# Low parts of five weight pairs moved from VectorE to GpSimd, block 4's Gram run one slot later, and its L read by another queue

## The chip, the cores and the metric

The kernel runs on one core of a Trainium2 chip. The metric is device time in microseconds (us) of one execution; lower is better. Engines are called TensorE (PE; its weight loads are PEld), VectorE (DVE), ScalarE (ACT), GpSimd (POOL) and SyncE (SP). Each runs its own instructions strictly in order and meets the others through semaphores. SP, ACT and POOL also issue DMAs, each from its own queue.

## What is computed

Two stages, float32 throughout. The first is a delta-rule linear attention over 4 batches x 8 heads, 768 positions and head size 48; the second is a two-layer network on its output, 384 to 2048 and back.

```
k_n = k / (norm(k) + 1e-06)
for t in range(S):
    y[t] = q[t] @ state
    state = state + beta[t] * outer(k_n[t], v[t] - k_n[t] @ state)
h = x @ w_in          # x: y of all heads, (3072, 384)
out = maximum(0.01 * h, h) @ w_out
```

## The kernel before

**Tiling.** The 768 positions are cut into 12 blocks of 64. In a block all recurrences are independent, so a block of attention is dense algebra: the Gram products of its keys and queries (`gram`, TensorE tile `pg`, line 307), the inverse of a unit triangular matrix by column elimination on VectorE (`inv`, tiles `T`, `tmp` and `L`, lines 388 and 393), and small products that carry the state on (`solve`, tiles `pz`, `pu`, `pk`, `pw`, `py`, `pc`). The feed-forward part (`ffn`) works on the block before: 16 column groups f, two to a weight pair. For each f, nine matmuls make `ph` (line 722), ScalarE writes `gh` from it and VectorE the rest `gl` (line 737), and six matmuls add into `po` (line 713).

**High and low parts.** From block 1 on, a float32 product is made of three rounded ones: high x high, high x low, low x high. So each weight pair j (0 to 7) exists as a high part, rounded by ScalarE in `cast` (line 182), and a low part, the difference, made in `lows` (line 189) by one 128x1536 subtraction. Block 0 uses the plain weights. f 6 and 7 of block 1 need the low part of pair 3, f 8 and 9 that of pair 4, and so on to pair 7.

**Shared buffers.** The unrounded weights of pairs 3 and 4 lie in buffers `c3` and `c4`. `square` (line 478) takes the same two buffers for A and B, the block-diagonal tiles of `solve` from block 2 on: ScalarE zeroes them (tile `sq`, line 482) once the low parts of pairs 3 and 4 have been read. The elimination's result T goes to DRAM as `td` and, transposed by a ScalarE copy (line 453), as `tt`; it comes back as A (from `tt`, line 520), B (from `td`, line 523) and `rt` (line 529). `pz` multiplies by A, `pu` by B.

**What sets the order.** A hand-written loop at the end of the kernel emits the work: within block n and slot s (17 slots), first a step of `ffn`, then weight work from the table `work`, then steps of `solve`, `inv` and `gram`, spread over slot ranges in the tables `SV`, `IV`, `GG` and `G4`. A scheduler then orders each engine's instructions by a simulated timeline; `behind(name)` holds the instructions of its block that run on the marked instruction's own engine behind that instruction. In block n runs the `solve` of block n+1 and the `inv` of block n+2. Block 1 also holds two Grams, of blocks 3 and 4; the later blocks hold one.

**Lines that the change touches.** `lows` (185 to 194), `gram` (276 to 353; the DMA queue of block 4's Gram is chosen in line 290, `queue = nc.gpsimd if n == GS * NGR else nc.sync`) and the table `G4` (852). Names in the trace: `w<-cg,w` is a low part, `gd<-gs` and `L<-gd` carry a Gram's triangle through DRAM to the elimination, `kq` is a block's keys and queries, `rq` the masked queries, `gm` the corners, `rv` values and state.

Of the kernel before, what the change touches and what calls it, by code (L numbers as in the profile page):

```python
# [9 lines left out]
F32 = mybir.dt.float32  # L10
# [5 lines left out]
ALU = mybir.AluOpType  # L16
# [9 lines left out]
GS = 2  # L26
NGR = NSEQ // GS
# [20 lines left out]
def delta_moe_kernel(ctx: ExitStack, tc, kq0, kqT, kv, qT, beta, cst, w_all, out, nblk):  # L48
# [10 lines left out]
    nc = tc.nc  # L59
# [33 lines left out]
    def of(x, n, g):  # L93
        return ring[x][(n * NGR + g) % NR[x]]
# [23 lines left out]
    def behind(name):  # L118

        return tc.issue_after(mark[name]) if name in mark else nullcontext()  # L120
# [29 lines left out]
    def after(inst):  # L150
        mark["gl"] = mark["dv"] = inst.ins
# [33 lines left out]
    def lows(j):  # L185
        g, t = parts[j]
        hi, lo = t[:, 0:4 * DO], t[:, 4 * DO:]
        with behind("dv"), behind("el2" if j > 2 else None):
            after(nc.vector.tensor_tensor(lo, g, hi.bitcast(F32), ALU.subtract))  # L189
        for y, part in enumerate((hi, lo)):  # L190
            for e in range(2):
                for x, w in enumerate((wi, wo)):
                    w[y][2 * j + e] = part[:, (2 * e + x) * DO:(2 * e + x + 1) * DO]

    Lh, gm, nrm, Tts, zs, ys, xs, done = {}, {}, {}, {}, {}, {}, {}, set()

    def need(gen, fn, n):
        while (fn, n) not in done:
            next(gen)
# [76 lines left out]
    def gram(n):  # L276
        need(sv, solve, n - Q_BUFS // NGR)
        kqs = []
        for g in range(NGR):
            t = sb.tile([P, GS, NPAIR, 2, C], F32, tag="kq", name=f"kq{n}_{g}", bufs=KQ_BUFS)  # L280
            kqs.append(t)
            with behind("kq"):
                for b in range(2):
                    nc.sync.dma_start(t[b * R0:b * R0 + D].rearrange("p s u x t -> p (s u x t)"), kqT[n, g, b])
        if n == GS:
            yield
        b0 = where[n][0]
        Lh[b0] = sb.tile([P, HC, HC], F32, tag="L", name=f"L{b0}", bufs=2)
        gd = dr.tile([64, HC, HC], F32, tag="gd", name=f"gd{n}")
        queue = nc.gpsimd if n == GS * NGR else nc.sync  # L290
        if n - 1 > 1 and where[n - 1][0] in nrm:
            with behind("ph"):
                lengths(n - 1)
        for g in range(NGR):
            kq = kqs[g]
            gs = sb.tile([P, 2, NPAIR, C], F32, tag="gs", name=f"gs{n}_{g}", bufs=2)
            if not g:
                gm[n] = sb.tile([P, GU, HC], F32, tag="gm", name=f"gm{n}", bufs=GM_BUFS)

            ps = [ps_a.tile([P, 512], F32, tag="a", name=f"pg{n}_{g}_{b}") for b in range(2)]  # L300
            pv = [x.rearrange("p (u x t) -> p x u t", u=NPAIR, x=2) for x in ps]
            for p in range(NPAIR):
                for c in range(2):
                    for b in range(2):
                        r = slice(b * R0, b * R0 + D)
                        with behind("ph") if n > 2 else nullcontext():
                            nc.tensor.matmul(ps[b][c * 64:(c + 1) * 64, p * 128:(p + 1) * 128],  # L307
                                             kq[r, c ^ b, p, 0], kq[r, c ^ b, p].rearrange("p x t -> p (x t)"),
                                             start=True, stop=True)
            for b in range(2):  # L310
                nc.scalar.copy(gs[:, b], pv[b][:, 0])  # L311
            for c in range(2):
                for e in range(2):
                    a = e * HS + g * GH + c * GU
                    queue.dma_start(
                        gd[a:a + GU].rearrange("l j i -> j l i"),
                        gs[c * 64 + e * HC:c * 64 + (e + 1) * HC].rearrange("p b u t -> p (b u) t")[:, :, e * HC:(e + 1) * HC])

            def masked(pv=pv, qa=of("q", n, g)):
                for b in range(2):  # L320
                    for c in range(2):
                        r = slice(c * 64, (c + 1) * 64)
                        with behind("gl") if n > 2 else nullcontext():
                            nc.vector.tensor_tensor(  # L324
                                qa[DN, c, b * NPAIR:(b + 1) * NPAIR], pv[b][r, 1],
                                tri[r].rearrange("p (o t) -> p o t", o=1).broadcast_to([C, NPAIR, C]), ALU.mult)

            def corners(g=g, gs=gs):
                for c in range(2):
                    k = 2 * g + c  # L330
                    with behind("gl") if n > 2 else nullcontext():
                        nc.vector.tensor_copy(gm[n][k * HC:(k + 1) * HC].rearrange("p (b u) t -> p b u t", b=2), gs[c * 64:c * 64 + HC, :, :, HC:])

            if n == 2:
                masked()
                corners()
            elif not g:
                masked()
                held.append(corners)
            else:  # L340
                tails.extend([[masked], held + [corners]])
                held.clear()
            if g == NGR - 1:
                for r in range(2):
                    i = queue.dma_start(Lh[b0][r * 64:(r + 1) * 64].rearrange("l j i -> l (j i)"), gd.rearrange("l j i -> l (j i)"))
                if n == GS * NGR:
                    mark["kq"] = i.ins
                done.add((gram, n))
            yield
# [53 lines left out]
    def inv(b):  # L403

        if b:
            need(gg, gram, NB[b][0])
# [159 lines left out]
    def lengths(n):  # L566

        b, i = where[n]
        ps = ps_a.tile([P, 512], F32, tag="a", name=f"pn{n}")
        nc.tensor.matmul(ps[DN, 0:HS], nrm[b][i * 64:i * 64 + 64], eye0[i * 64:i * 64 + 64], start=True, stop=True)  # L570
        nt = nts[n] = sb.tile([P, NGR, 2, GU], F32, tag="nt", name=f"nt{n}", bufs=2)
        if n < 2:
            for y in range(2):
                nc.scalar.copy(nt[DN, :, :, y * NPAIR:(y + 1) * NPAIR],
                               ps[DN, y * GH:(y + 1) * GH].rearrange("p (g h v) -> p g h v", g=NGR, h=2))
        else:
            nc.scalar.copy(nt[DN].rearrange("p g h u -> p (g h u)"), ps[DN, 0:HS])
        if not n:
            for g in range(NGR):
                v = of("v", n, g)  # L580
                for u in range(GU):
                    for c in range(2):
                        nc.scalar.mul(v[DN, c, u], v[DN, c, u], nt[DN, g, c, u:u + 1])
# [190 lines left out]
    def weave_at(i, n, *streams):  # L774

        for gen, steps, a, b in streams:
            key = gen, n, a
            want = steps if i >= b - 1 else min(steps, max(0, i + 1 - a) * steps // (b - a))
            while taken.get(key, 0) < want:
                next(gen, None)  # L780
                taken[key] = taken.get(key, 0) + 1
# [5 lines left out]

    NS, NF, NI = NSLOT, NFC + 1, HC + 1
    fg, gg = first(), chain(gram, range(2, nblk))
    iv = chain(inv, range(len(NB)))  # L790
    sv = chain(solve, range(nblk))
# [19 lines left out]
    lo, hi = slice(0, 1), slice(1, 2)  # L811
# [3 lines left out]
    for j in (4, 5):  # L815
# [7 lines left out]
        2: ((load_w, 6, "dv"), (conv, 3), (final, 2), (pack, 4, "h0_2")),  # L823
        3: ((expand, 3, "h0_3"),),
        4: ((load_w, 7, "dv"), (conv, 4), (final, 3), (cast, 0, "h0_4"), (lows, 0)),
        5: ((expand, 4, "h0_5"), (pack, 5, "h0_4")),
        6: ((conv, 5), (final, 4), (cast, 1, "h0_6"), (lows, 1)),
        7: ((expand, 5, "h0_7"), (pack, 6, "h0_6")),
        8: ((conv, 6), (final, 5), (cast, 2, "h0_8"), (lows, 2)),
        9: ((expand, 6, "h0_9"), (pack, 7, "h0_8")),  # L830
        10: ((conv, 7), (final, 6),),
# [5 lines left out]
    for n in range(nblk):  # L837

        for s in range(NF):
            at = min(n, 3)  # L840
            weave_at(s, n, (ff, NF, 0, NF))
            for fn, *args in work.pop(n * NF + s, ()):
                fn(*args)
            weave_at(s, n, (sv, (NS + (n == 0)) * (n + 1 < nblk), *SV[at]), (iv, NI * (n + 2 < nblk), *IV[at]),
                     (gg, NGR * (n < 2), *GG[min(n, 1)]), (gg, NGR * (0 < n < nblk - 3), *G4[min(n, 2)]))

# [2 lines left out]
WARM = {HC - 12: 16}  # L849
KA = 2  # L850
IV, GG = ((9, 17), (6, 17), (2, 17), (2, 17)), ((2, 4), (1, 2))
G4 = (0, 1), (13, 14), (12, 13)
SV = (0, 10), (3, 13), (1, 11), (2, 12)
PD, FB = 2, 4

# [65 lines left out]
```

## Time and profile before

| | |
|---|---|
| median of 3 runs | 621.96 us (621.48 to 624.78) |
| the profiled execution | 626.66 us, its span 624.7 us |
| PE busy | 584.0 us (93%) |
| PEld busy | 537.3 us (86%) |
| DVE busy | 431.4 us (69%) |
| ACT busy | 330.6 us (53%) |
| POOL busy | 39.5 us (6%) |

The span runs from the first to the last instruction; the execution's own time is 2.0 us longer. Busy shares are means over stages with different limits, so they are read stage by stage. [...]

### The profile page before, as it was taken

The page shows a single profiled execution, that of the slowest core. Times are in us where ns is not written, and L with a number is a line of the kernel's source. Part 1 is how long each engine was busy: PE and PEld are TensorE (multiplying, and loading weights), DVE is VectorE, ACT ScalarE, POOL GpSimd, SP SyncE. Part 2 cuts the span into 40 slices and gives each one's busy share as a digit, 9 for nine tenths or more (in the row PEclk, how much of TensorE's full clock was granted, in tenths as well). Part 3 has the DMA queues.
Part 4 walks back from the last instruction along what each step waited for, and adds up shares of the span by engine and source line. Part 5 has one row for each costly group of instructions (what it writes and reads, how often), then busy time and mean ns, then how long its engine had stood idle before and what let it go on. Part 6 is the DMA issues. An engine that isn't in the chain of part 4 may idle for free.

```text
span 624.7 us, 22338 instructions
## 1 busy us (share of the span) xinstructions
PE 584.0 (93%) x9122; PEld 537.3 (86%) x9122; DVE 431.4 (69%) x1949; ACT 330.6 (53%) x818; POOL 39.5 (6%) x71
## 2 busy tenths in 40 slices
PE   5278989889899999999999999999999999999996
PEld 4266767688799999999999999999999999999996
DVE  3998899968648859759759739749759659331212
ACT  3377976635435536545545536545545545454432
POOL 6000000100130010010010010010010010100100
PEclk9989999989789999999999999999999999999999
DMA  5985933261470462571480570580570550500101
GB/s 127 321 249 219 290 78 79 57 115 19 98 162 9 94 135 39 104 142 24 104 149 16 112 139 19 114 149 6 117 148 7 116 94 4 87 26 4 25 1 26
DMA packets 120102, 59.69 MB, mean 96 GB/s; under 512 B 109248, under 2 KB 110336, under 8 KB 118976
## 3 DMA queue, kind: packets, MB, share of 16 engines
q1 hardware_dynamic: 116896, 52.42, 38.7%
q0 software_dynamic: 2528, 5.12, 3.3%
q8 instruction: 72, 1.18, 0.8%
q10 hardware_dynamic: 576, 0.72, 0.6%
q14 instruction: 30, 0.25, 0.1%
HBM read 46.96 MB, written 11.27 MB: 93 GB/s over the span
## 4 chain that ended last, share of the span: by engine, by line
PE 80%; DVE 13%; issue 3%; DMA 2%; ACT 1%; SPq 0%; DVEq 0%; ACTq 0%
PE po L713 31%; PE ph L722 31%; PE pk L619 3%; PE pw L636 3%; PE pg L307 3%; DVE T L393 3%; PE py L656 3%; DVE tmp L388 3%; PE pc L646 2%; DVE w L189 1%; DVE cg L175 1%; PE px L691 1%; PE pu L490 1%; PE pz L490 1%; DMA kx<-in_kq 1%
## 5 line engine op out<-in xcount | busy, mean ns | idle before, releaser
L722 PE MATMUL ph<-xh,w 128*128 128x256 f32 x1056 | 207.1, 287 | 0.0
L713 PE MATMUL po<-w,gh 128*128 128x384 f32 x704 | 179.1, 346 | 0.0
L722 PEld LDWEIGHTS ph<-xh,w 128*128 128x128 f32 x1056 | 170.3, 191 | 4.5 <-issue 3.7
L737 DVE TENSOR_TENSOR gl<-ph,gh 128x256 fp32r<-128x256 f32 x176 | 74.0, 421 | 141.6 <-ACT ph L736 135.0
L732 ACT ACTIVATE gh<-ph 128x256 fp32r<-128x256 f32 (+1 forms) x192 | 73.5, 385 | 181.4 <-PE ph L722 131.5
L722 PE MATMUL ph<-xl,w 128*128 128x256 f32 x528 | 149.3, 285 | 1.7 <-DVE xl L124 1.7
L713 PEld LDWEIGHTS po<-w,gh 128*128 128x128 f32 x704 | 122.0, 190 | 3.4 <-issue 2.0
L713 PE MATMUL po<-w,gl 128*128 128x384 f32 x352 | 113.6, 344 | 2.4 <-DVE gl L737 2.3
L393 DVE TENSOR_TENSOR T<-T,tmp 128x60 f32<-128x60 f32 (+35 forms) x661 | 112.4, 207 | 0.7
L388 DVE TENSOR_TENSOR tmp<-T,L 128x60 f32<-128x60 f32 (+35 forms) x661 | 112.1, 208 | 0.6
L722 PEld LDWEIGHTS ph<-xl,w 128*128 128x128 f32 x528 | 100.6, 191 | 2.4 <-DVE xl L124 2.1
L713 PEld LDWEIGHTS po<-w,gl 128*128 128x128 f32 x352 | 66.0, 190 | 4.0 <-DVE gl L737 3.4
L736 ACT ACTIVATE ph<-ph 128x256 f32<-128x256 f32 x176 | 66.8, 380 | 0.0
L764 POOL DMA_DIRECT2D out<-ob x44 | 23.0, 528 | 492.9 <-ACT ob L763 492.3
L324 DVE TENSOR_TENSOR rq<-pg,csb 64x256 f32<-64x256 f32 x80 | 33.8, 423 | 6.6 <-ACT gs L311 5.1
L621 ACT ACTIVATE rt<-pk 48x512 f32<-48x512 f32 x44 | 26.1, 593 | 6.3 <-PE pk L619 5.5
L648 ACT COPY rv<-pc 48x384 f32<-48x384 f32 x44 | 20.9, 475 | 13.0 <-PE pc L646 12.6
L722 PE MATMUL ph<-x,cg 128*128 128x256 f32 x96 | 22.8, 385 | 3.4 <-DVE cg L175 1.9
L638 ACT COPY rv<-pw 64x384 f32<-64x384 f32 x48 | 22.7, 474 | 6.0 <-PE pw L636 4.8
L722 PEld LDWEIGHTS ph<-x,cg 128*128 128x128 f32 x96 | 17.7, 190 | 8.1 <-DVE cg L175 3.4
L307 PE MATMUL pg<-kq 48*64 48x128 f32 x640 | 24.0, 284 | 0.0
L636 PEld LDWEIGHTS pw<-rv,rt 128*32 128x32 f32 x1536 | 19.0, 114 | 5.3 <-ACT ph L736 2.1
(101 smaller groups left out, 610.1 us busy)
## 6 DMA issues: line engine op xcount, KB each, us to landing
wr<-in_w_all SPq DMA_DIRECT2D x8, 1536.0 KB, 14.2
kq<-in_kqT SPq DMA_DIRECT2D x40, 192.0 KB, 4.8
rk<-in_kv SPq DMA_DIRECT2D x24, 192.0 KB, 3.8
rv<-in_kv SPq DMA_DIRECT2D x24, 192.0 KB, 3.9
rq<-in_qT SPq DMA_DIRECT2D x24, 192.0 KB, 3.7
L<-gd SPq DMA_DIRECT2D x18, 256.0 KB, 4.3
out<-ob POOLq DMA_DIRECT2D x44, 96.0 KB, 2.5
td<-T SPq DMA_DIRECT2D x40, 64.0 KB, 3.0
```

The source lines that it names most:

```text
L307: nc.tensor.matmul(ps[b][c * 64:(c + 1) * 64, p * 128:(p + 1) * 128], kq[r, c ^ b, p, 0], kq[r, c ^ b, p].rearrange("p x t -> p (x t)"), s ...
L324: nc.vector.tensor_tensor(qa[DN, c, b * NPAIR:(b + 1) * NPAIR], pv[b][r, 1], tri[r].rearrange("p (o t) -> p o t", o=1).broadcast_to([C, NP ...
L388: nc.vector.tensor_tensor(tv, t[:, :, j:j + 1].broadcast_to([P, k, w]), L[:, j, j + 1:].rearrange("p (o w) -> p o w", o=1).broadcast_to([P ...
L393: mark["steps"] = nc.vector.tensor_tensor(t, t, tv, ALU.subtract).ins
L621: nc.scalar.mul(t[UP, c], pv[c * 64:c * 64 + D].rearrange("p (y v) t -> p y v t", y=2), -1.0)
L636: nc.tensor.matmul(pv[a:a + HC, u], t[:, c, u // NPAIR, u % NPAIR, e * HC:(e + 1) * HC], v[:, c, u], start=True, stop=True)
L713: i = nc.tensor.matmul(po[t][:, :DO], a[:, ts_], w, start=(f == 0 and k == 0), stop=(f == NFC - 1 and k + 1 == len(ways)))
L722: i = nc.tensor.matmul(ph, w[:, cc * P:(cc + 1) * P], a, start=(k == 0), stop=(k + 1 == len(ways)))
L732: i = nc.scalar.activation(gh, ph, AF.Prelu, alpha=0.01)
L736: i = nc.scalar.activation(ph, ph, AF.Prelu, alpha=0.01)
L737: mark["gl"] = nc.vector.tensor_tensor(gl, ph, gh.bitcast(F32), ALU.subtract).ins
L764: nc.gpsimd.dma_start(out[r0:r0 + C], ob[a:a + C])
```

## The change

It does four things. Low parts of pairs 3 to 7 are subtracted by GpSimd; VectorE only clears one column of each first, and that small write is held behind the last subtraction that block 2's inverse emits, so that GpSimd's subtraction waits for it. Block 4's Gram is emitted in slot 14 of block 1 and no longer in slot 13. Its `L` is read back by SyncE, while its `gd` is still written by GpSimd. And block 5's `kq` loads carry a different `behind` mark (`h2_4`, which marks a ScalarE instruction).

```diff
--- before.py
+++ after.py
@@ -185,8 +185,13 @@
     def lows(j):
         g, t = parts[j]
         hi, lo = t[:, 0:4 * DO], t[:, 4 * DO:]
-        with behind("dv"), behind("el2" if j > 2 else None):
-            after(nc.vector.tensor_tensor(lo, g, hi.bitcast(F32), ALU.subtract))
+        if j > 2:
+            with behind("el2"):
+                nc.vector.memset(lo[:, 0:1].bitcast(F32), 0.0)
+            nc.gpsimd.tensor_tensor(lo, g, hi.bitcast(F32), ALU.subtract)
+        else:
+            with behind("dv"):
+                after(nc.vector.tensor_tensor(lo, g, hi.bitcast(F32), ALU.subtract))
         for y, part in enumerate((hi, lo)):
             for e in range(2):
                 for x, w in enumerate((wi, wo)):
@@ -279,7 +284,7 @@
         for g in range(NGR):
             t = sb.tile([P, GS, NPAIR, 2, C], F32, tag="kq", name=f"kq{n}_{g}", bufs=KQ_BUFS)
             kqs.append(t)
-            with behind("kq"):
+            with behind("h2_4" if n == GS * NGR + 1 else "kq"):
                 for b in range(2):
                     nc.sync.dma_start(t[b * R0:b * R0 + D].rearrange("p s u x t -> p (s u x t)"), kqT[n, g, b])
         if n == GS:
@@ -342,7 +347,7 @@
                 held.clear()
             if g == NGR - 1:
                 for r in range(2):
-                    i = queue.dma_start(Lh[b0][r * 64:(r + 1) * 64].rearrange("l j i -> l (j i)"), gd.rearrange("l j i -> l (j i)"))
+                    i = nc.sync.dma_start(Lh[b0][r * 64:(r + 1) * 64].rearrange("l j i -> l (j i)"), gd.rearrange("l j i -> l (j i)"))
                 if n == GS * NGR:
                     mark["kq"] = i.ins
                 done.add((gram, n))
@@ -849,7 +854,7 @@
 WARM = {HC - 12: 16}
 KA = 2
 IV, GG = ((9, 17), (6, 17), (2, 17), (2, 17)), ((2, 4), (1, 2))
-G4 = (0, 1), (13, 14), (12, 13)
+G4 = (0, 1), (14, 15), (12, 13)
 SV = (0, 10), (3, 13), (1, 11), (2, 12)
 PD, FB = 2, 4
```

VectorE at the end of block 2's inverse (`T_1483`, `tmp_29`, `tmp_30` are its last steps; `gl_0`, `gl_1` belong to block 1), before:

```order
L189 TENSOR_TENSOR w_1687<-cg_1211,w_1687 128x1536
L189 TENSOR_TENSOR w_1745<-cg_1278,w_1745 128x1536
L189 TENSOR_TENSOR w_1747<-cg_1443,w_1747 128x1536
L388 TENSOR_TENSOR tmp_29_0_1767<-T_1483,L_1075 128x16
L737 TENSOR_TENSOR gl_0_1810<-ph_72,gh_0_1808 128x256
L324 TENSOR_TENSOR rq_80<-pg_0_0_1834,csb 64x256 x2
L324 TENSOR_TENSOR rq_80<-pg_0_1_1835,csb 64x256 x2
L393 TENSOR_TENSOR T_1483<-T_1483,tmp_29_0_1767 128x8x2
L737 TENSOR_TENSOR gl_1_1816<-ph_72,gh_1_1814 128x256
```

and with the change:

```order
L190 MEMSET w_1687 128x1
L190 MEMSET w_1745 128x1
L190 MEMSET w_1747 128x1
L393 TENSOR_TENSOR tmp_29_0_1767<-T_1483,L_1075 128x16
L398 TENSOR_TENSOR T_1483<-T_1483,tmp_29_0_1767 128x8x2
L393 TENSOR_TENSOR tmp_30_0_1773<-T_1483,L_1075 128x8
L398 TENSOR_TENSOR T_1483<-T_1483,tmp_30_0_1773 128x8
L742 TENSOR_TENSOR gl_0_1810<-ph_72,gh_0_1808 128x256
L742 TENSOR_TENSOR gl_1_1817<-ph_72,gh_1_1815 128x256
```

The five long subtractions have become five one-column writes, and the last elimination steps now stand ahead of `gl_0`. GpSimd's own row, which before held only block 0's output, the Gram's `gd` and the output of block 1 here, is with the change:

```order
L110 COPY rk_77<-csb 64x768
L769 DMA out<-ob_0_1737 64x384 x2
L769 DMA out<-ob_1_1741 64x384 x2
L191 ISA
L191 TENSOR_TENSOR w_1621<-cg_966,w_1621 128x1536
L191 TENSOR_TENSOR w_1657<-cg_1025,w_1657 128x1536
L191 TENSOR_TENSOR w_1687<-cg_1211,w_1687 128x1536
L191 TENSOR_TENSOR w_1745<-cg_1278,w_1745 128x1536
L191 TENSOR_TENSOR w_1747<-cg_1443,w_1747 128x1536
L320 DMA gd_2622<-gs_0_2627 32x8x32 x4
L320 DMA gd_2622<-gs_1_2657 32x8x32 x4
```

The five subtractions stand behind block 0's output, with one instruction (`ISA`) ahead of them that the program before does not have there, and ahead of block 4's `gd`.

TensorE late in block 1 (`ph`, `po` with weights `w_1687`, `w_1745`, `w_1747` are pairs 5 to 7), before:

```order
L722 MATMUL ph_73<-xh_0_1721,w_1747 128x256
L722 MATMUL ph_73<-xh_1_1725,w_1747 128x256
L722 MATMUL ph_73<-xl_1_1726,w_1747 128x256
L656 MATMUL py_0_2355<-rv_84,rq_78 32x48 x30
L656 MATMUL py_1_2390<-rv_85,rq_79 32x48 x32
L646 MATMUL pc_0_2472<-rv_84,rk_76 48x48 x16
L646 MATMUL pc_1_2491<-rv_85,rk_77 48x48 x16
L570 MATMUL pn_2571<-csb,sq_2059 64x32
L307 MATMUL pg_0_0_2577<-kq_0_2563 64x128 x8
L722 MATMUL ph_73<-xh_1_1725,w_1747 128x256
L722 MATMUL ph_73<-xh_2_1729,w_1747 128x256
```

and with the change, where `pc` of the same solve stands:

```order
L718 MATMUL po_0_1788<-w_1687,gh_10_2320 128x384 x2
L718 MATMUL po_0_1788<-w_1687,gl_10_2322 128x384
L718 MATMUL po_1_1789<-w_1687,gh_10_2320 128x384 x2
L718 MATMUL po_1_1789<-w_1687,gl_10_2322 128x384
L651 MATMUL pc_0_2477<-rv_84,rk_76 48x48 x16
L651 MATMUL pc_1_2496<-rv_85,rk_77 48x48 x16
L718 MATMUL po_0_1788<-w_1687,gh_11_2349 128x384 x2
L718 MATMUL po_0_1788<-w_1687,gl_11_2351 128x384
L718 MATMUL po_1_1789<-w_1687,gh_11_2349 128x384 x2
L718 MATMUL po_1_1789<-w_1687,gl_11_2351 128x384
```

Earlier in the same queue, at the start of f 6 of block 1, with the change:

```order
L727 MATMUL ph_73<-xl_0_1722,w_1621 128x256
L727 MATMUL ph_73<-xh_0_1721,w_1621 128x256
L727 MATMUL ph_73<-xh_1_1725,w_1621 128x256
L727 MATMUL ph_73<-xl_1_1726,w_1621 128x256
L727 MATMUL ph_73<-xh_1_1725,w_1621 128x256
L495 MATMUL pz_1984<-sq_1972,gm_1078 32x128 x8
L727 MATMUL ph_73<-xh_2_1729,w_1621 128x256
L727 MATMUL ph_73<-xl_2_1730,w_1621 128x256
L727 MATMUL ph_73<-xh_2_1729,w_1621 128x256
```

The solve of block 2 moves forward: `pz` stood in the middle of `po` of f 7, and stands now between the matmuls of f 6 (`w_1621` is pair 3), and `py` and `pc` are now apart, with `ph` and `po` between them.

SyncE from block 2's T (`T_1483`) to A and B (`sq`), before:

```order
L315 DMA gd_1827<-gs_0_1832 32x8x32 x4
L315 DMA gd_1827<-gs_1_1862 32x8x32 x4
L284 DMA kq_1_2566<-in_kqT 48x1024 x2
L345 DMA L_1826<-gd_1827 64x1024 x2
L460 DMA td_1780<-T_1483 32x16x32 x2
L461 DMA tt_1781<-T_1483 1024x1x16
L460 DMA td_1780<-T_1483 32x16x32 x2
L461 DMA tt_1781<-T_1483 1024x1x16
L529 DMA rt_82<-td_1780 32x16x32
L529 DMA rt_83<-td_1780 32x16x32
L523 DMA sq_1970<-td_1780 32x8x32
L520 DMA sq_1968<-tt_1781 32x8x32 x4
```

and with the change:

```order
L465 DMA td_1780<-T_1483 32x16x32 x2
L466 DMA tt_1781<-T_1483 1024x1x16
L465 DMA td_1780<-T_1483 32x16x32 x2
L466 DMA tt_1781<-T_1483 1024x1x16
L289 DMA kq_0_2615<-in_kqT 48x1024
L534 DMA rt_82<-td_1780 32x16x32
L320 DMA gd_1829<-gs_0_1834 32x8x32 x4
L320 DMA gd_1829<-gs_1_1864 32x8x32 x4
L525 DMA sq_1972<-tt_1781 32x8x32 x2
L350 DMA L_1828<-gd_1829 64x1024 x2
L525 DMA sq_1972<-tt_1781 32x8x32 x2
L528 DMA sq_1974<-td_1780 32x8x32 x4
```

T's stores have moved ahead of block 3's `gd` and `L`, which now stand between them and A. One block later block 4's `L` stands in this queue behind A, B, `rt` and block 5's `kq`; before, that `kq` stood behind `rt` too, and that `L` was on GpSimd's queue.

## Rows read from the trace of the kernel before

**Rows 1.** busy time by stretch: us, PE, PEld, DVE, ACT, POOL, clock, DMA

```profile
114.69:178.32 63.63, 56.98 (x794) 52.30 (x793) 49.23 (x209) 29.63 (x74) 6.65 (x12) 0.89 0.43 82
270.20:316.00 45.80, 45.80 (x730) 43.17 (x729) 33.94 (x173) 24.19 (x64) 2.06 (x4) 1.00 0.46 91
128.00:132.00 4.00, 3.57 (x18) 3.57 (x19) 3.82 (x12) 1.40 (x3) 0.00 (x0) 0.59 0.90 217
160.00:164.00 4.00, 1.84 (x92) 1.65 (x82) 3.82 (x33) 1.05 (x3) 0.00 (x0) 1.00 0.46 102
166.00:174.00 8.00, 8.00 (x66) 7.45 (x66) 2.95 (x9) 3.27 (x9) 2.78 (x5) 0.50 0.84 146
```

**Rows 2.** timeline of TensorE, block 1: start, us, what, idle before

```profile
115.88 0.39 PE L722 MATMUL ph<-xl,w 128*128 128x256 f32 x1 [0.50 <-DVE xl L124]
...
118.91 0.38 PE L722 MATMUL ph<-xl,w 128*128 128x256 f32 x1 [1.20 <-DVE xl L124]
...
126.00 0.62 PE L713 MATMUL po<-w,gl 128*128 128x384 f32 x2 [1.25 <-DVE gl L737]
...
128.43 1.01 PE L713 MATMUL po<-w,gl 128*128 128x384 f32 x2 [1.04 <-DVE gl L737]
...
163.37 0.97 PE L646 MATMUL pc<-rv,rk 128*48 128x48 f32 x34 [2.16 <-issue]
```

**Rows 3.** chain that ended last, one steady block: start, us, what

```profile
260.50 1.83 PE pg L307 x59
...
263.59 2.15 PE ph L722 x18
265.74 2.11 PE po L713 x12
```

**Rows 4.** timeline of VectorE, end of block 2's inverse

```profile
116.77 1.75 DVE L189 TENSOR_TENSOR w<-cg,w 128x1536 fp32r<-128x1536 f32 x1
...
118.77 6.75 DVE L189 TENSOR_TENSOR w<-cg,w 128x1536 fp32r<-128x1536 f32 x4
...
127.74 0.18 DVE L393 TENSOR_TENSOR T<-T,tmp 128x16 f32<-128x16 f32 x1
```

**Rows 5.** timeline of GpSimd, start and end of block 0

```profile
9.68 1.59 POOL L110 COPY rk<-csb 64x768 f32<-64x768 f32 x2
...
117.18 1.04 POOL L764 DMA_DIRECT2D out<-ob  x2 [0.68 <-ACT ob L763]
```

**Rows 6.** timeline of VectorE, two transposes

```profile
9.92 1.97 DVE L246 STREAM_TRANSPOSE L<-S 128x1024 f32<-128x1024 f32 x1
...
37.08 2.03 DVE L439 STREAM_TRANSPOSE tc<-T 128x1024 f32<-128x1024 f32 x1
```

**Rows 7.** DMA issues: KB each, median us from issue to landing

```profile
wr<-in_w_all SPq DMA_DIRECT2D x8, 1536.0 KB, 14.2
...
L<-gd SPq DMA_DIRECT2D x18, 256.0 KB, 4.3
...
sq<-tt SPq DMA_DIRECT2D x40, 32.0 KB, 2.0
...
L<-gd POOLq DMA_DIRECT2D x2, 256.0 KB, 7.2
```

**Rows 8.** timeline of ScalarE, block 1

```profile
118.62 1.06 ACT L482 ACTIVATE sq<-csb 128x1024 f32<-128x1024 f32 x1 [1.73 <-DVE w L189]
...
133.72 0.38 ACT L732 ACTIVATE gh<-ph 128x256 fp32r<-128x256 f32 x1 [0.49 <-DVE gl L737]
```

**Rows 9.** timeline of SyncE's queue, block 1

```profile
123.17 3.78 SPq L315 DMA_DIRECT2D gd<-gs  x8
...
128.21 1.09 SPq L345 DMA_DIRECT2D L<-gd  x2
131.25 0.86 SPq L460 DMA_DIRECT2D td<-T  x2
...
137.84 2.02 SPq L520 DMA_DIRECT2D sq<-tt  x4
```

## The prediction

> **What bounds the kernel now.** I read the busy time by stretch first. A steady block lasts 45.80 us and TensorE is busy in all of it; block 1, from its first `ph` to that of block 2, lasts 63.63 us, in which TensorE is busy 56.98 at a mean granted clock of 0.89 [rows 1]. A block with one Gram more should cost the 45.80 and a Gram's 1.83 [rows 1, 3]: 47.6. So block 1 is 16.0 us too long, and it is the block that the change works on. The 16.0 are 63.63 - 56.98 = 6.65 of waiting, 63.63 x (1 - 0.89) = 7.0 of clock, and 2.35 that no row names.
>
> The timeline of TensorE says what it waits for: 0.50 and 1.20 for `xl`, 1.25 and 1.04 for `gl`, all VectorE's, and 2.16 in the middle of `pc` for nothing that the profile shows [rows 2]. The timeline of VectorE has the cause of all but the first and the last: five subtractions of low parts, 1.75 + 6.75 = 8.5 us in a row, and behind them the end of block 2's inverse, which reaches `td` only at 131.25 [rows 4, 9]. [...]
>
> **What the change removes.** VectorE loses the 8.5 us [rows 4]; the five one-column writes that stay hold one element each and I count them as nothing, since VectorE is then ahead. T of block 2 is complete 12.8 us sooner, at about 118.4 in place of 131.2: without the row that begins at 118.77, the four short last steps, 0.18 each [rows 4], follow `xl` at once. The order shows the solve pulled forward with it and `py` and `pc` spread between `ph` and `po`, as they lie in the steady blocks, where TensorE does not wait. So all of the 16.0 can go except the first 0.50, which hangs on `xl` as before: 15.5. The 2.35 that no row names may be seams of the moved products or may stay; bounds 0 and 2.35, I let half stay: -14.3.
>
> **What it adds.** First GpSimd's time. Its last output issue ends at 118.2 [rows 5]. Then comes an instruction (`ISA`) that the trace does not show; bounds are nothing and 14.2 us, the slowest transfer of the page, and I take 7.2, the slowest that GpSimd itself issued, as the nearest [rows 7]. A subtraction of 1536 columns: GpSimd copies 768 in 0.80 us, 1.59 for two [rows 5], so one operand alone is 1.6 us, the lower end; two operands in turn make 3.2, which I take; twice that, 6.4, is the upper end. The low part of pair 3 is then ready at 118.2 + 7.2 + 3.2 = 128.6, and those of pairs 4 to 7 every 3.2 us, until 141.4.
>
> Who waits for that? TensorE asks for pair 3 late. From 114.69: 0.50 of waiting, 36 matmuls of `ph` (4.30), the Gram (2.0), `po` of f 0 and 1 (2.11), `ph` of f 4 and 5 (2.15) make 125.75, and `po` of f 2 and 3 still lies before pair 3 [rows 1, 2, 3]. But ScalarE zeroes A only after pair 3's low part is read, since both share a buffer; before, it waited 1.73 for the same reason, and the zeroing took 1.06 [rows 8]. `gh` of f 2 stands behind it. Zeroed at 128.6 + 1.06 = 129.7, then three steps of 0.38 (`gh`, the second activation, `gl`) give `gl` at 130.8 [rows 8]. TensorE would be there at 125.75 + 0.35 = 126.1 and loses **4.7**.
>
> Second, SyncE's queue. `pz` now stands behind six matmuls of f 6: 130.8 + 1.76 + 0.72 = 133.3 [rows 3]. A is loaded by four issues of 0.5 us, with two issues of `L`, 1.09, in their middle; from 129.7 the last is out at 132.8 and lands 2.0 later, at 134.8 [rows 7, 9]. TensorE loses **1.5**. Had GpSimd cost nothing, A would still be late: the way from T's first store to A's last issue was 131.25 to 139.86, 8.6 us; `gd` and `L` now stand in it, 3.78 + 1.09 and 1.3 of waiting between them, about 1 us of B and `rt` has moved out [rows 9]: 118.4 + 8.6 + 6.1 - 1.0 + 2.0 = 134.1, while TensorE reaches `pz` at 128.6, a wait of 5.5. So the two delays cover each other: 6.2 together, 5.5 at least.
>
> Third, the clock. After the two waits for `gl`, 2.3 us together, the clock was 0.59 over 4 us, a loss of 1.6 [rows 1, 2]; 6.2 us of waiting will bring that once: **1.6**. It might bring none, or the 4.0 that 8 us at 0.50 cost [rows 1].
>
> Three edits come out at nothing. The Gram in slot 14 is the same work a little later, with TensorE busy on both sides of it. `L` of block 4 now stands in SyncE's queue behind A, B, `rt` and `kq`; before, GpSimd's issue took 7.2 us to land and SyncE's takes 4.3 [rows 7], which pays for about 3 us of standing. If that cover fails, VectorE stands at the norms of block 4 with `gl` of f 4 behind it, and each us late is one on TensorE, 3 at most. The third edit does not do what its words say: `h2_4` marks an instruction of ScalarE, so it holds nothing on SyncE, and the order has block 5's `kq` where it was.
>
> **Sum.** -14.3 + 4.7 + 1.5 + 1.6 = -6.5 us, against the profiled execution of 626.66: 620.2. That execution is 4.7 above the median of the three runs; the difference carries over, so 621.96 - 6.5 = **615.5**.
>
> [...]
>
> **The rivals.** *The delays are covered.* If GpSimd is near its lower ends and A's loads run closer together than I lay them, TensorE keeps its pace and only some of the 15.5 is given back. For it: the two delays hang on five queue steps that I put in a row, and in steady blocks TensorE does not wait for A. Against it: `gd` and `L` stand before A in order, and that part is certain. It gives 606.5 with nothing lost, 611 with half of it: chance 0.20.
>
> *VectorE is shut out while GpSimd reads.* If GpSimd's subtractions hold a way into SBUF that VectorE needs, VectorE's copies of the corners (`gm`, four, right behind `gl` of f 3 and ahead of `gl` of f 4) can each wait out one subtraction. `gl` of f 3 comes at about 133; the subtractions end at 135.0, 138.2 and 141.4, so `gl` of f 4 comes at 142.4, while TensorE needs it at 137.2, 0.57 of `pz`, 1.43 of `ph` and 0.35 of `po` after A's landing [rows 3, 7]. That costs 5.2 and another 1.6 of clock: -6.5 + 6.8 = +0.3, 622.3, no change. From there each us that a subtraction is longer than 3.2 costs about 5, since five stand in a row, so it is **slower** from 3.8 us on, and at 4.3 it is 628. This is the case on the other side. For it: GpSimd is busy 16 us or more exactly where VectorE has eight short steps that `gl` waits behind. Against it: at the start, a transpose on VectorE beside GpSimd's copies took 1.97 us, and a like one alone 2.03 [rows 5, 6], no slower; but it reads one operand only.
>
> [...]
>
> **Chances.** My forecast 0.48; covered 0.20; shut out and no change 0.20; shut out or a late library instruction, and slower 0.12. A measurement of this kernel can tell about 0.5%, 3.1 us, from no change. The forecast ends up within that in about one case in twelve (GpSimd's instruction at its upper end costs 7 more), so faster 0.64, same 0.24, slower 0.12. The range reaches from 607.5, nearly all covered, to 625.0, shut out with subtractions somewhat over 3.2; a tenth is left outside at either end. Faster cases alone would span 607.5 to 618.5.
>
> **What would show it.** Right: block 1 shrinks from 63.6 to about 57; VectorE has no 1.75 us steps at 117 to 125; T's first store is issued near 118.5; TensorE's wait of 2.16 in `pc` and the 8 us at 0.50 are gone; there is a wait of 3 to 6 us in all before `po` of f 2 or 3 and at `pz`, put down to `gl`, ScalarE's zeroing or A's DMA. Wrong: GpSimd's five rows last under 2 or over 4.5 us; `gm` copies begin exactly as those rows end; the wait at `pc` stays; TensorE waits for pairs 5 to 7 themselves; or the steady blocks change their 45.8.

## The result and the profile after

The changed kernel took **629.44 us** (median of 4 runs, 627.16 to 630.93) where the kernel before took 622.89 beside it (4 runs, 621.48 to 624.78): a ratio of **1.0101**, 95% interval 1.0065 to 1.0136. It is slower by about 1%; 615.5 had been predicted, with a range up to 625.0.

The profiled execution of the changed kernel took 628.08 us, its span 626.2. Its busy time by stretch: the first three rows are blocks 1, 2 and 3, each from its first `ph` to that of the next block; then come three short stretches behind waits, and block 2 of the kernel before for comparison. Columns as in [rows 1]; the clock is the one that was granted to TensorE, as a share of its full speed.

```profile
114.22:171.05 56.83, 51.22 (x797) 47.62 (x796) 48.30 (x202) 27.95 (x72) 21.17 (x12) 0.94 0.36 67
171.05:224.96 53.91, 49.68 (x730) 46.54 (x729) 36.05 (x179) 24.86 (x66) 5.07 (x9) 0.94 0.51 99
224.96:272.41 47.45, 45.80 (x730) 43.12 (x730) 33.84 (x172) 24.18 (x64) 2.08 (x4) 1.00 0.44 86
134.00:139.00 5.00, 4.67 (x31) 4.32 (x32) 2.86 (x6) 1.62 (x5) 1.01 (x1) 0.50 0.82 161
190.00:194.00 4.00, 3.82 (x65) 3.68 (x66) 3.78 (x11) 3.38 (x10) 0.00 (x0) 0.53 0.00 0
194.00:198.00 4.00, 4.00 (x18) 3.68 (x19) 4.00 (x28) 1.69 (x4) 0.00 (x0) 0.62 0.03 4
```

```profile
178.32:224.75 46.43, 46.43 (x732) 43.72 (x731) 33.97 (x173) 23.66 (x64) 3.43 (x7) 1.00 0.40 84
```

Block 1 is as short as was forecast: 56.83 us, where the profile of before had 63.63 [rows 1] and the prediction named about 57. The time is lost behind it. Cut in the same way, blocks 2 and 3 took 46.43 and 45.71 in that profile; they take 53.91 and 47.45 now. Block 2 holds 53.91 - 49.68 = 4.2 us of waiting, and 53.91 x (1 - 0.94) = 3.2 of clock: TensorE ran at 0.53 and 0.62 for the 8 us from 190 on. The waits, in the timeline of TensorE:

```profile
115.42 0.39 PE L727 MATMUL ph<-xl,w 128*128 128x256 f32 x1 [0.50 <-DVE xl L124]
...
134.33 1.08 PE L495 MATMUL pz<-sq,gm 128*32 128x128 f32 x16 [5.11 <-DMA sq<-tt]
...
190.18 3.63 PE L624 MATMUL pk<-rt,rk 64*48 64x64 f32 x64 [4.12 <-ACT rt L557]
...
233.16 0.64 PE L495 MATMUL pz<-sq,gm 128*32 128x128 f32 x16 [1.65 <-DMA L<-gd]
```

Of the five waits of [rows 2] only the 0.50 for `xl` is left. In their place stands one of 5.11 at the `pz` in block 1 (the solve of block 2), for A's loads. The 4.12 before `pk` in block 2 and the 1.65 at the `pz` in block 3 are new. VectorE has the cause of the 4.12, and ScalarE hands it on:

```profile
125.68 10.38 DVE L337 COPY gm<-gs 32x256 f32<-32x256 f32 x4
136.08 0.42 DVE L742 TENSOR_TENSOR gl<-ph,gh 128x256 fp32r<-128x256 f32 x1
...
187.07 0.19 DVE L369 TENSOR_SCALAR sr<-L 128x32 uint32<-128x32 uint32 x1 [7.99 <-DMA L<-gd]
...
188.26 0.42 DVE L742 TENSOR_TENSOR gl<-ph,gh 128x256 fp32r<-128x256 f32 x1
```

```profile
188.71 0.38 ACT L737 ACTIVATE gh<-ph 128x256 fp32r<-128x256 f32 x1 [6.92 <-DVE gl L742]
...
189.39 1.49 ACT L557 COPY rt<-pu 32x256 f32<-32x256 f32 x4
```

The burst of 1.75 and 6.75 [rows 4] is gone. But VectorE stands 7.99 us at the norms of block 4 (`sr`), which need its `L`, and `gl` of f 4 is queued behind them. ScalarE's `gh` of f 5 waits 6.92 for that `gl`, the copy of `rt` that `pk` needs stands behind that `gh`, and TensorE waits 4.12. The queue of SyncE says why `L` came late:

```profile
117.51 1.24 SPq L465 DMA_DIRECT2D td<-T  x2
...
122.62 4.81 SPq L320 DMA_DIRECT2D gd<-gs  x8
127.53 0.89 SPq L525 DMA_DIRECT2D sq<-tt  x2
...
176.72 1.73 SPq L534 DMA_DIRECT2D rt<-td  x3
178.49 1.51 SPq L289 DMA_DIRECT2D kq<-in_kqT  x3
180.31 1.13 SPq L350 DMA_DIRECT2D L<-gd  x2
```

`L` of block 4 is issued at 180.31, behind `rt` and three loads of block 5's `kq`, and is there 6.8 later. The first three rows are the 5.11 at `pz`: block 2's T is stored from 117.51 on, 13.7 us sooner than before, but A is first issued at 127.53, right behind block 3's `gd`. GpSimd did its part:

```profile
116.72 1.03 POOL L769 DMA_DIRECT2D out<-ob  x2 [0.66 <-ACT ob L768]
117.85 17.16 POOL L191 TENSOR_TENSOR w<-cg,w 128x1536 fp32r<-128x1536 f32 x5
```

The output issue has ended at 117.75 and the first subtraction starts at 117.85, so the `ISA` instruction cost nothing that can be seen; five last 17.16, or 3.43 each, and end at 135.01. The corner copies of blocks 3 and 4, grouped (count, then shortest, median and longest in ns, then the first and last start):

```profile
L337 DVE COPY gm<-gs x8: 282/285/9483, 125.7 to 176.8; 32x256 f32<-32x256 f32 x8
```

A copy takes 0.28 us; the first, at 125.7, took 9.48, until GpSimd's last subtraction had ended. `gl` of f 4 stood behind it until 136.08, and ScalarE's next `gh` waited 9.39. VectorE was shut out, as in the second rival. TensorE stood at `pz` for 5.11 of these 10 us anyway, and had other matmuls in the rest.

### The profile page after: what moved, and what is told of

Its sections match the earlier page's. It is cut to its first block, busy times and chain, and to the rows that moved or that the text cites. A ratio compares the mean times of both kernels' runs of the same rounds, so it can differ in the third digit from the quotient of the medians.

```text
span 626.2 us, 22354 instructions
## 1 busy us (share of the span) xinstructions
PE 581.6 (93%) x9122; PEld 535.8 (86%) x9122; DVE 432.4 (69%) x1949; ACT 329.8 (53%) x818; POOL 55.6 (9%) x74
## 4 chain that ended last, share of the span: by engine, by line
PE 75%; DVE 12%; DMA 5%; ACT 3%; SPq 3%; issue 2%; DVEq 0%; ACTq 0%
PE po L718 29%; PE ph L727 29%; PE pk L624 3%; PE pw L641 3%; DVE T L398 3%; DVE tmp L393 3%; PE py L661 3%; PE pc L651 2%; PE pg L312 2%; DMA L<-gd 2%; PE pz L495 1%; PE px L696 1%; DMA gd<-gs 1%; PE pu L495 1%; DVE cg L175 1%
## 5 line engine op out<-in xcount | busy, mean ns | idle before, releaser
L624 PEld LDWEIGHTS pk<-rt,rk 64*48 64x48 f32 x704 | 21.8, 127 | 7.2 <-ACT rt L557 4.3
L624 PE MATMUL pk<-rt,rk 64*48 64x64 f32 x704 | 23.5, 226 | 4.1 <-ACT rt L557 4.1
```

The costliest lines, as they stand in the source:

```text
L624: nc.tensor.matmul(pv[r, u], k[DN, c, u], t[DN, c, u // NPAIR, u % NPAIR], start=True, stop=True)
```

## The experiments

Each edit is against the changed kernel, if nothing else is said. Ratios are to the kernel before in the same session (621.86 to 622.47 us); differences are of medians, and by the ratios those to the changed kernel are about 1 us smaller. Three theories: **(1)** the way of block 4's `L` costs the time; **(2)** the copies that GpSimd shuts out do; **(3)** A's loads, late behind `gd` and `L` of block 3, do. A `pz` "in block n" is the one that runs in block n, for the solve of block n+1. The diffs show the lines that matter.

### One edit taken back or made alone

**lows_alone**: the kernel before, with only `lows` of the change.

> The kernel before with the first edit alone: the low parts of pairs 3 to 7 by GpSimd, block 4's Gram in slot 13 and its L issued by GpSimd as before. Theory 1 (the change loses on the way of block 4's L: Gram a slot later, L on SyncE behind A, B, rt and kq, so that VectorE stands 8 us at the norms with gl behind it, which costs TensorE 4.1 us of waiting and 3.4 of clock): block 1 is as short as in the changed kernel, about 59 us from ph to ph, the wait before pk of 4.1 is gone, and the time is 629.4 - 7.5 = 622 or less, down to 618 if block 3's wait of 1.65 goes too. Theory 2 (VectorE's corner copies shut out for 10 us by GpSimd's subtractions are the loss): nothing of that changes, 628 to 631. Theory 3 (A's loads, late behind gd and L of block 3 on SyncE, are the loss): the wait of 5.1 at pz stays, and the time with it, 628 to 631.

Measured 621.88, ratio 0.9988 (0.9957 to 1.0018). The wait before `pk` is gone, 4.84 at `pz` stays, and there is a wait of 1.09 at the `pz` in block 3. Theory 1 holds; but without the loss the first edit alone is worth nothing that can be measured.

**lows_by_vector**: the reverse, the subtractions back on VectorE.

```diff
-        if j > 2:
-            with behind("el2"):
-                nc.vector.memset(lo[:, 0:1].bitcast(F32), 0.0)
-            nc.gpsimd.tensor_tensor(lo, g, hi.bitcast(F32), ALU.subtract)
...
+        with behind("dv"), behind("el2" if j > 2 else None):
+            after(nc.vector.tensor_tensor(lo, g, hi.bitcast(F32), ALU.subtract))
```

> The changed kernel with the low parts back on VectorE: the Gram in slot 14 and L of block 4 by SyncE stay. Theory 1: block 1 is as long as before, about 63.6 us, and the late L adds to it wherever gl of block 2 stands behind the norms: 625 to 631, slower than the kernel before. Theories 2 and 3 (the loss lies in GpSimd's subtractions, or in T of block 2 that comes sooner and sends A behind gd): without the subtractions on GpSimd neither is there, so the time is that of the kernel before, 621 to 624.

Measured 625.87, ratio 1.0050 (1.0024 to 1.0077), with 3.26 us of waiting before `pk` and 6.79 of VectorE at the norms. Without any subtraction on GpSimd, the other edits alone make the kernel slower. Theories 2 and 3 cannot do that. The loss is smaller here, some 4 us: block 2 takes 52.59, but the wait in block 3 is not there. Block 1 takes 58.72, not the 63.6 that was expected.

**L_by_gpsimd**:

```diff
-                    i = nc.sync.dma_start(Lh[b0][r * 64:(r + 1) * 64].rearrange("l j i -> l (j i)"), gd.rearrange("l j i -> l (j i)"))
+                    i = queue.dma_start(Lh[b0][r * 64:(r + 1) * 64].rearrange("l j i -> l (j i)"), gd.rearrange("l j i -> l (j i)"))
```

> The changed kernel with one word put back: L of block 4 is issued by GpSimd again, the Gram stays in slot 14. TensorE's order is that of the changed kernel; on VectorE the norms of block 4 move behind one more pair of gl. Theory 1: L is issued when gd has landed, near 177 in place of 180.3, and lands near 184, and gl no longer stands behind the norms: the wait of 4.1 before pk falls to 1 or less and the clock there does not drop, so 629.4 - 7.5 = 622, to 625 if half stays. Theories 2 and 3: 628 to 631, since block 1 is not touched.

Measured **619.60**, ratio 0.9956 (0.9935 to 0.9977): 9.8 us under the changed kernel, and under the kernel before too. The wait before `pk` is gone. But one step of the expectation fell. The norms do not come much sooner:

```profile
182.51 0.42 DVE L742 TENSOR_TENSOR gl<-ph,gh 128x256 fp32r<-128x256 f32 x1 [2.73 <-ACT ph L741]
183.66 0.42 DVE L742 TENSOR_TENSOR gl<-ph,gh 128x256 fp32r<-128x256 f32 x1 [0.72 <-ACT ph L741]
184.12 1.97 DVE L632 TENSOR_TENSOR rv<-rv,nt 64x384 f32<-64x384 f32 x4
186.18 0.19 DVE L369 TENSOR_SCALAR sr<-L 128x32 uint32<-128x32 uint32 x1
```

That is VectorE's timeline of this run. The norms start at 186.18, only 0.9 before the 187.07 of the changed kernel. `L`'s two transfers, issued by GpSimd from 178.46 on, took a median of 5.8 us to land, as SyncE's two in the changed kernel did (5.8). What differs is the order: `gl` of f 4 and f 5 stand ahead of `sr`, and nobody waits. The scheduler had put `sr` ahead of `gl` of f 4 when SyncE issued `L`, so `L` was late for a place in the queue and not for its own use.

**gram_slot_13**: the table back to `(13, 14)`, `L` still by SyncE.

> The changed kernel with block 4's Gram back in slot 13; L stays on SyncE, but now stands ahead of rt there. Theory 1 with the slot as its cause: L lands about 2.5 us sooner after gd, the norms come sooner on VectorE, and the wait of 4.1 before pk falls to under 2: 622 to 625. Theory 1 with the queue as its cause: L still stands behind A's and B's loads, VectorE still waits 5 us or more at the norms with gl behind: 627 to 631. Theories 2 and 3: 628 to 631.

Measured 621.63, ratio 0.9987 (0.9967 to 1.0008). `L` is issued at 178.08, ahead of `rt`, VectorE waits 4.04 at the norms and TensorE 0.81. With the third edit in both, slot 14 without SyncE's queue (L_by_gpsimd) and SyncE's queue without slot 14 (this run) cost nothing that can be measured; together they cost 8 us. The next run takes out the third edit.

**kq_behind_kq**: the third edit taken back, the one that the prediction counted as without effect.

```diff
-            with behind("h2_4" if n == GS * NGR + 1 else "kq"):
+            with behind("kq"):
```

> The changed kernel with the third edit alone taken back: block 5's kq stands behind block 4's L in SyncE's queue again, where it stood three loads of 1.5 us ahead of it. Theory 1 (how late L is issued sets the loss): L lands about 1.5 us sooner, VectorE's wait at the norms falls from 8.0 to about 6.5 and TensorE's before pk from 4.1 to about 2.6: 627 to 628 of 629.4. Rival (A's and B's loads ahead of L set it, or the transfer itself, not the issue): no change, 629 to 630.

Measured 621.05, ratio 0.9986 (0.9955 to 1.0017): 8.4 us less than the changed kernel, where 1.5 to 2.5 had been expected. TensorE's order is the same as in the changed kernel. SyncE's queue in this run, then VectorE, then TensorE with the stretch around its wait:

```profile
177.33 1.18 SPq L534 DMA_DIRECT2D rt<-td  x2
178.83 1.13 SPq L350 DMA_DIRECT2D L<-gd  x2
...
182.47 1.76 SPq L289 DMA_DIRECT2D kq<-in_kqT  x4
```

```profile
183.80 0.19 DVE L369 TENSOR_SCALAR sr<-L 128x32 uint32<-128x32 uint32 x1 [4.13 <-DMA L<-gd]
...
185.38 0.36 DVE L742 TENSOR_TENSOR gl<-ph,gh 128x256 fp32r<-128x256 f32 x1
```

```profile
187.24 1.99 PE L624 MATMUL pk<-rt,rk 64*48 64x64 f32 x64 [0.61 <-ACT rt L557]
```

```profile
186.00:190.00 4.00, 3.39 (x75) 3.11 (x74) 3.77 (x13) 3.85 (x12) 0.00 (x0) 1.00 1.07 174
```

`L` is issued 1.5 us sooner and, with no `kq` ahead of it, is there 5.0 after its issue and not 6.8: 3.3 us sooner in all. VectorE waits 4.13 in place of 7.99, TensorE 0.61 before `pk` in place of 4.12, and the clock from 186 to 190 is 1.00. So 3.3 us of `L` were worth 3.5 of waiting, the 3.2 of clock that hung on that wait (block 2 has a mean clock of 1.00 here and had 0.94), and the 1.65 of block 3: 8.35 together, about what the medians show. So the loss takes all three edits, the slot, the queue and the mark of `kq`: with any one of them taken back it is gone. That `kq` ahead of `L` is what made the landing 1.8 longer (medians of the two transfers 5.8 and 4.0) is inferred from the order of the queue; the edit moves both.

### The kernel before, profiled again

**before_again**: no edit.

> The kernel before, unchanged, with a second profile. The profiled execution that the prediction started from lies 4.7 us above the median of its kernel. Theory a: that excess lies in block 1 (the 2.16 us in the middle of pc for nothing that the profile shows, the clock behind it, and seams): then blocks 1 and 2 together last 105 to 106 us here in place of 110.1, and the ceiling of 15.5 us that the prediction took from that profile was some 4.7 too high for a typical execution. Theory b: the excess is spread over the whole program or lies outside block 1: then blocks 1 and 2 last 109 us or more again.

One run, 621.80. Blocks 1 and 2 and two of the stretches of [rows 1]:

```profile
113.80:172.30 58.50, 52.44 (x795) 47.98 (x794) 48.09 (x206) 28.59 (x72) 3.98 (x7) 0.97 0.41 80
172.30:219.14 46.84, 46.84 (x731) 43.79 (x731) 34.86 (x176) 24.14 (x66) 6.04 (x11) 1.00 0.46 93
...
160.00:164.00 4.00, 2.66 (x80) 2.34 (x75) 3.01 (x27) 2.03 (x5) 0.00 (x0) 1.00 0.43 123
166.00:174.00 8.00, 8.00 (x79) 7.45 (x72) 5.76 (x17) 4.40 (x13) 2.83 (x5) 1.00 0.71 120
```

Theory a holds. Block 1 lasts 58.50, not 63.63, and both blocks 105.3, not 110.1. The waits for `gl` of 1.26 and 1.04 are the same, the wait in `pc` is 1.34 and not 2.16, and after it TensorE runs at 1.00 where the first profile had 0.50. Most of the 4.7 us by which that execution lay above its median were that low clock, in block 1: 8 us at 0.50 are 4.0.

### What still bounds block 1

**L_corners**: `L` of block 4 by GpSimd, and the corner copies of block 3 by ScalarE.

```diff
-                        nc.vector.tensor_copy(gm[n][k * HC:(k + 1) * HC].rearrange("p (b u) t -> p b u t", b=2), gs[c * 64:c * 64 + HC, :, :, HC:])
+                        (nc.scalar.copy if n == 3 else nc.vector.tensor_copy)(gm[n][k * HC:(k + 1) * HC].rearrange("p (b u) t -> p b u t", b=2), gs[c * 64:c * 64 + HC, :, :, HC:])
```

> The changed kernel with L of block 4 issued by GpSimd, and with the four corner copies of block 3 (gm, 32x256) moved from VectorE to ScalarE. Theory: VectorE's copies are shut out while GpSimd subtracts, but TensorE stands at pz for A's loads during nearly all of that, so the lock costs nothing: gl of f 4 is there at about 127 in place of 136.6, the wait of 5.1 at pz stays, and the time is that of the run with L by GpSimd alone, 618 to 621. Rival: the lock is a second cause of the low clock and of waits behind pz: 616 or less. If ScalarE's copies are held up in the same way, gl of f 4 comes late as before.

Measured 620.88, ratio 0.9984 (0.9959 to 1.0010). `gl` of f 4 is done at 127.5 and no longer at 136.5, ScalarE's copies take 0.41 each beside GpSimd, and the wait at `pz` is 5.31 (a new one of 1.2 stands at the `pz` in block 2). So in the changed kernel the shut-out costs nothing: it lies under the wait for A.

**gram3_slot_4**: `L` of block 4 by GpSimd, and block 3's Gram later.

```diff
-IV, GG = ((9, 17), (6, 17), (2, 17), (2, 17)), ((2, 4), (1, 2))
+IV, GG = ((9, 17), (6, 17), (2, 17), (2, 17)), ((2, 4), (4, 5))
```

> The changed kernel with L of block 4 issued by GpSimd, and with block 3's Gram in slots 4 and 5 of block 1 in place of 1 and 2. A's loads then stand ahead of gd and L of block 3 in SyncE's queue, and the corner copies come after GpSimd's subtractions. Theory (gd and L ahead of A are what pz waits for, and the half clock follows from that wait): the wait of 5.1 at pz goes, and with it about 1.5 of clock: 619.6 - 6.6 = 613. Rival: the inverse of block 3, whose L now lands about 14 us later, ends later by some of that, and the wait turns up at the pz or ph of block 2: 617 to 624.

Measured 627.48, ratio 1.0097 (1.0064 to 1.0130). The wait at `pz` in block 1 is gone, and three things take its place. VectorE's `rv` products, 0.55 each, take 5.80 for four, the first of them 4.39, until GpSimd's last subtraction is done; `pu` waits 3.44 for nothing that the profile names, and no run here told what for; and block 3's inverse, later by its Gram, brings a wait of 2.70 at the `pz` in block 2. The rival holds.

**A_by_scalar**: `L` of block 4 by GpSimd, and A's four loads for block 2 from ScalarE's queue.

```diff
-                nc.sync.dma_start(A[r, :, r], Tt[k * GU:(k + 1) * GU].rearrange("u i m -> i u m"))
+                (nc.scalar if n == 2 else nc.sync).dma_start(A[r, :, r], Tt[k * GU:(k + 1) * GU].rearrange("u i m -> i u m"))
```

> The changed kernel with L of block 4 issued by GpSimd, and with the four loads of A for block 2's pz issued from ScalarE's queue instead of SyncE's, so that gd and L of block 3 no longer stand ahead of them. The corner copies stay on VectorE. Theory (two delays lie over each other at pz: A behind gd and L, and the corner copies that GpSimd's subtractions shut out until 135): A lands near 128, but pz also reads the corners, so it starts near 136 all the same, put down to VectorE's gm, and the time is 619 to 621 as with L by GpSimd alone. Rival (A's loads alone are what pz waits for; the lock only looks long): pz starts near 129 and the time is 613 to 615.

Measured 619.34, ratio 0.9957 (0.9929 to 0.9986), the same as without it. `pz`, which the scheduler now puts into the middle of a `po`, starts at 128.24 without a wait, so the expectation had the wrong place: these copies are block 3's and this `pz` does not read them. But they stand ahead of `gl` of f 4, and that is where TensorE now waits. First TensorE, then VectorE:

```profile
128.24 0.64 PE L495 MATMUL pz<-sq,gm 128*32 128x128 f32 x16
...
136.23 0.69 PE L718 MATMUL po<-w,gl 128*128 128x384 f32 x1 [4.32 <-DVE gl L742]
```

```profile
128.63 7.09 DVE L337 COPY gm<-gs 32x256 f32<-32x256 f32 x4
135.76 0.42 DVE L742 TENSOR_TENSOR gl<-ph,gh 128x256 fp32r<-128x256 f32 x1
```

**A_corners**: both edits, A's loads and block 3's corner copies by ScalarE, with `L` of block 4 by GpSimd.

> Both at once: the loads of A from ScalarE's queue, and the corner copies of block 3 on ScalarE; L of block 4 by GpSimd. Theory: with both delays gone pz starts near 129, the wait of 5.1 and the half clock behind it go, 619.6 - 6.6 = 613. Rival 1: ScalarE now has four issues and four copies ahead of gh of f 2 and f 3, so TensorE waits for gl there and gives back 2 to 3 of it: 615 to 617. Rival 2: B's loads on SyncE, or T's transposed part, come late for pu in place of A's for pz, and the time stays at 619 to 621.

Measured **614.26**, ratio **0.9873** (0.9841 to 0.9905), the fastest of all. Its blocks 1 and 2:

```profile
114.40:166.08 51.68, 49.88 (x796) 45.71 (x795) 38.96 (x198) 29.65 (x76) 21.29 (x12) 1.00 0.45 89
166.08:212.68 46.60, 46.48 (x730) 43.49 (x730) 35.09 (x179) 24.06 (x66) 6.23 (x11) 1.00 0.47 93
```

Block 1 falls to 51.68 at a clock of 1.00. Either delay taken away alone changes nothing (619.34 and 620.88, of 619.60); both together give 5.3 us. They lay over each other.

**late_L_A_corners**: A_corners, with `L` of block 4 by SyncE again, as in the change.

> The changed kernel with A's loads of block 2 from ScalarE's queue and block 3's corner copies on ScalarE, and with L of block 4 left where the change puts it, on SyncE behind A, B, rt and kq. Theory (the late L is a cost of its own, independent of what happens at pz): the wait of some 4 us before pk in block 2 comes back with the low clock behind it, and the time is 614.3 + 8 to 10 = 622 to 624. Rival (the late L only matters because block 1's end had been delayed by the wait at pz): 614 to 617.

Measured 625.73, ratio 1.0051 (1.0024 to 1.0078): 11.5 us more, for one word. VectorE waits 7.74 at `sr`, TensorE 3.88 before `pk`, 1.48 in block 3 and 2.68 at `pu`. The late `L` is a cost of its own; its size was expected too low, and `pu` accounts for part of the difference.

**vector_A_corners**: A_corners, with the subtractions back on VectorE.

> The low parts back on VectorE, with everything else as in the fastest kernel so far: A's loads and the corner copies by ScalarE, L of block 4 by GpSimd, the Gram in slot 14. Theory (moving the subtractions to GpSimd is what pays, once A and the corners are out of its way): VectorE's 8.5 us of subtractions stand ahead of T of block 2 again, the waits for gl of 1.2 us each and the pile of pw, py and pc come back, and the time is that of the kernel before, 620 to 623. Rival (the loads and copies by ScalarE pay by themselves): 614 to 617.

Measured 628.69, ratio 1.0112 (1.0055 to 1.0168): 14.4 us more than A_corners. The waits for `gl` of 1.26 and 1.03 are back. In block 1 ScalarE, with A's four issues in its queue, stands 5.56 at them, since T is late there; `gl` and block 3's inverse queue behind that on VectorE, so block 3's T is stored from 171.46 on, 5.1 us later than in before_again, and 3.03 of waiting stand at the `pz` in block 2. So the loads by ScalarE do not pay by themselves, and with them GpSimd's subtractions do.

## Why the prediction was wrong

**The ceiling.** That "all of the 16.0 can go except the first 0.50" was read from one execution, 4.7 above the median, and the step "the difference carries over" failed. It did not carry over: the second profile of the same kernel has block 1 at 58.5, so the 4.7 were in the very stage that was to be saved. By that second profile block 1 is 10.9 too long, not 16.0. That the low clock at its end (0.50 from 166 to 174, behind 4 us in which TensorE was busy 1.84 [rows 1]) would go with the late solve was an estimate; in the second profile, with the solve in the same order, it is 1.00. The forecast -6.5 was right against the profile that it was made from (63.63 to 56.83, -6.8), and is -1.7 against the other one; the four runs that only take the late `L` back (lows_alone, L_by_gpsimd, gram_slot_13, kq_behind_kq) came out 0.1 to 2.4 under the kernel before. What it named as signs for block 1 came: T's store at 117.51, no waiting in `pc`, one wait of 3 to 6 us at `pz`.

**GpSimd.** The subtraction was put at 3.2 and took 3.43. The `ISA` term of 7.2 is nothing here: 117.85 follows the end of the output issue at 117.75. So the 4.7 for the squares did not come about; ScalarE waited 0.58 for GpSimd at the second zeroing.

**A's loads.** The term of 1.5 was mis-sized, with 5.11 measured; the prediction's own bound for a GpSimd that costs nothing was 5.5, and GpSimd's `ISA` instruction did cost nothing that shows (0.10 from the output issue to the first subtraction). The sum of the two terms, 6.2, hid that the first was too high and the second too low: that block 1 came out as forecast is in that part luck.

**The clock.** A loss of 1.6 was put behind that wait: from 134 to 139 the clock was 0.50, and TensorE was busy 4.67 of that, a loss of 2.3. The place was right, the size somewhat low. A second one, behind the wait before `pk`, was not foreseen.

**The step that failed most** is "Three edits come out at nothing". Of `L` it said that 4.3 in place of 7.2 to land "pays for about 3 us of standing" and that VectorE, if that cover fails, would cost "3 at most". VectorE stood 7.99, TensorE 4.12, and the clock cost 3.2 on top. The place was right (the norms, with `gl` of f 4 behind them), the size was not: `L` was there 6.8 after its first issue (the two transfers took a median of 5.8), the clock behind a wait was counted for `pz` and not for this one, and a wait of 1.65 in block 3 came with it. Of the third edit it said that it "does not do what its words say" and leaves `kq` where it was. The comparison was with the wrong kernel. The old mark is the issue of block 4's `L` itself; with that issue on SyncE the old mark would have sent `kq` behind `L`. Leaving `kq` where it was is what the edit does, and the run without it is 8.4 us faster. This 8.4 and the 4.7 of the ceiling are the 13.1 us between the -6.5 that was forecast and the +6.5 that was measured.

**The rival of the shut-out** came about: a copy that takes 0.27 to 0.29 us in the kernel before, where VectorE subtracts (all 40 of them), takes 9.48 and lasts until GpSimd is done. It waited for all that was left of the run of subtractions, where the rival had it wait for one. What it said about the place was right too, `gl` of f 4, and it costs 4.32 at once where A is early (A_by_scalar). In the changed kernel it is hidden under the wait for A, and a subtraction stayed under the 3.8 from which the rival was to be slower: the kernel came out slower, but for none of the reasons that the prediction gave to that case.

## What to carry to other kernels

A transfer that moves to another queue, or behind other loads there, can also move its consumer in the order of the engine that waits for it, as `sr` moved ahead of `gl` of f 4 here: look at what stands behind that consumer, and price its whole queue with the clock that follows the wait (7.99 on VectorE, 4.12 on TensorE and 3.2 of clock in this case). An edit that leaves the order as it was may still matter, when another edit would have changed it (8.4 here); compare with the kernel that lacks this edit alone. And where the profiled execution lies above the median, profile a second one before the saving is counted, since the excess may lie in the stage that is to be saved (block 1 took 63.63 in one execution and 58.50 in the other).

## What was not expected of the hardware

**VectorE was not served between two of GpSimd's subtractions.** In the changed kernel the first `gm` copy began at 125.7, in the third of five subtractions of 3.43 us, and took 9.48, until the fifth had ended. Three ended in that time, and the copy got its turn after none but the last: it sat through the two behind the one that it began in as well. In gram3_slot_4 a product of two SBUF operands, `rv`, was held in the same way for 4.39 us, where the other three of that group took 0.55 each. The products that read one operand from PSUM ran at their usual pace beside GpSimd in the changed kernel: `gl` took 0.42, the mean of all 176, and the masks `rq` 1.73 for four, where each of the 80 in the kernel before took 0.42 to 0.43. What it is that held the one kind and let the other pass, no run here shows.

**What the clock was behind a wait.** Behind 5.11 at `pz` the granted clock was 0.50 for the next 4.7 us, and behind 4.12 at `pk` 0.53 and 0.62 for 8; behind 0.61 at `pk` in kq_behind_kq it was 1.00, while two waits of 2.3 together had brought 0.59 [rows 1, 2]. In two executions of the kernel before, the same 8 us at the end of block 1 ran once at 0.50 and once at 1.00.
